# Splitting the first blocks' exponentials by slot under a new issue order, in a gated linear recurrence with an MLP mixer

## The chip, the cores and the metric

The kernel runs on one core of a Trainium2 chip. The metric is device time in microseconds (us) of the whole launch. Before the change it was 166.19 us, the median of three runs (165.96 to 166.21).

## What is computed

For each of 4 batches and 8 heads a 48 by 48 state is carried over 768 positions, and its output feeds a mixer of two matrix pairs, the first over positions ("token"), the second over the 384 features ("channel"):

```python
for t in range(S):                                   # S = 768
    state = alpha[:, :, t, :, None] * state + np.einsum('bhd,bhe->bhde', k[:, :, t], v[:, :, t])
    y[:, :, t] = np.einsum('bhd,bhde->bhe', q[:, :, t], state)
x = y as (batch, 768, 8 * 48)
h = np.maximum(x.transpose(0, 2, 1) @ w_tok1, 0.0) @ w_tok2
u = x + h.transpose(0, 2, 1)
out = u + np.maximum(u @ w_ch1, 0.0) @ w_ch2
```

## The kernel before, in words

**Blocks.** Each batch has 768 positions, worked in three blocks of 256, so there are 12 blocks, numbered 0 to 11. A block lies on 128 partitions in two slots: partition p holds positions 2p (slot 0) and 2p + 1 (slot 1) of all heads. For each block four loads of 384 KB fetch alpha (`ld_at`), k (`ld_kt`), q (`ld_qt`) and v (`ld_vt`). They go into 20 buffers called `in`. Six further pieces each of `wc1` and `wc2`, and two each of `wt1` and `wt2`, are the mixer's weights. They are fetched into the same buffers (`ldw_...`) and cast to bf16 (`cw_...`).

**The recurrence of a block.** ScalarE (ACT) takes the logarithm of alpha. TensorE (PE) multiplies it by triangular matrices, which gives running sums in PSUM (`cumw` for the first three blocks, `cum` for the others). ACT takes their exponential E and the exponential IE of the negative. q times E (`qq` for slot 1, `ql` for slot 0; tile pkq) and k times IE (`kk`, `kl`; tile pkk) are made on VectorE (DVE) or GpSimd (POOL). PE transposes both (`trq`, `trk`), an engine copies them out of PSUM (`evq`, `evk`), PE multiplies them (`G0_`, `G1_`), DVE applies the causal mask while it copies out (`mask0_`, `mask1_`; tile gtm, line 720), and PE multiplies by v (`y0_`, `y1_`). The state comes in by `K`, `sa`, `s0_`/`sm` and `ia`/`ib`. The result is copied to `x0_`, `x1_`. `vb` and `vs` cast v. The blocks 0, 1 and 2 (`WIDE` in the code) take both slots through the sums. The others first multiply the two slots of alpha (`P`) and need `lnP`, `ln1`, `r1`, `k0a` and `q0r`.

**The mixer of a batch.** When the three blocks of a batch have given six x tiles, come `t1` (token, first matrix), `ht` (relu), `t2`, `u` (adding x), a transpose of u (`up`/`ut` on PE for batches 0 and 1, a transposing DMA `ux` for 2 and 3), 24 groups `c1` of three matmuls, each with its relu `rt` on ACT or DVE, 24 groups `c2`, an add `o` on DVE, and a store `st`. In the last batch one output tile is cut into 320 columns (`h0`) and 64 columns (`h1`).

**What sets the order.** All operations, their engine and the order on each engine stand in one table of names, `ORDER`, and the buffers in a second table, `BUFS`. The last letter of an entry is its engine: t PE, s ACT, v DVE, g POOL, y SyncE (SP), which only issues DMAs. ACT issues those with the letter s. Every engine works through its entries in order, so an entry that waits holds all behind it. A method `shared` adds one more wait: where DVE and POOL take turns in a marked list of operations (products, casts and copies between SBUF tiles, in the table's order), the first on the new engine waits for the last on the other.

**Unread products.** Entries `f1_...` and `f3_...` are one or three matmuls of zeros into a bank that the named operation overwrites afterwards. Nothing reads them.

Of the kernel before, what the change touches and what calls it, by code (L numbers as in the profile page):

```python
# [380 lines left out]
kk2g vs0_1g ldw_wt11s y1_0t evq2v G0_1t ia1t kk3g f1_G11t ldw_wt20y ldw_wt21y mask0_1v k0a3g x1_0s G1_1t ld_kt4y vb2s
trk2t mask1_1v ldw_wc10y r13s ib1t K2t evk2s sa0_2t sm0_2v G0_2t cw_wt10s mask0_2v kl3g ldw_wc11y vs1_1g vs0_2g vs1_2s
ka3s vb3s f3_G12t G1_2t kb3s ldw_wc13y t1_0_1_0t y0_1t trk3t ld_at5y y1_1t cw_wt11g ib2t ia2t ln14s mask1_2v y0_2t
x0_1v x0_2v x1_1s vs1_3s vs0_3s ld_qt4s ldw_wc12y kc3g t1_0_1_1t y1_2t t1_0_0_0t t1_0_1_2t P4g t1_0_0_1t t1_0_0_2t
t1_0_0_3t t1_0_0_4t q0r3g x1_2v t1_0_0_5t t1_0_1_3t evk3v qq3g t1_0_1_4t ql3g lnP4s t1_0_1_5t k0a4g ht_0_0s cw_wt20s
K3t ht_0_1v cum4t cw_wt21s t2_0_0t t2_0_1t IE4s s0_3v sa1_3v u_0_0v t2_0_2t kk4g ldw_wc15y trq3t u_0_1v u_0_2v t2_0_3t
t2_0_5t kl4g E4s evq3s up_0_0t t2_0_4t u_0_3v cw_wc10s u_0_5v u_0_4v up_0_1t ut_0_1s ut_0_0v ld_vt4y G1_3t G0_3t
up_0_2t ib3t mask0_3v mask1_3v trk4t ldw_wc14y c1_0_0_0t c1_0_1_0t cw_wc11g ut_0_2s c1_0_2_0t c1_0_3_1t r14s cw_wc13s
ldw_wc21y c1_0_7_1t evk4s y1_3t y0_3t rt_0_1_0v q0r4v ka4v qq4v ql4g x0_3s x1_3v rt_0_0_0v rt_0_2_0v P5g cw_wc15g
c1_0_7_0t c1_0_6_1t rt_0_7_0s rt_0_7_1s cw_wc12s rt_0_3_1s c1_0_0_1t ld_qt5y c1_0_6_0t trq4t c1_0_2_1t c1_0_4_1t  # L390
ld_kt5y ldw_wc22y sm1_3g cw_wc14g vb4g lnP5s c1_0_10_1t evq4s ldw_wc20s rt_0_0_1s rt_0_6_0v rt_0_6_1v ld_vt5s
rt_0_2_1s c1_0_11_1t c1_0_11_0t rt_0_10_1v cum5t rt_0_11_1v G0_4t G1_4t kb4s IE5s rt_0_4_1v cw_wc21g kc4g ln15s E5s
c1_0_10_0t c1_0_3_0t r15s rt_0_10_0s c1_0_9_1t vs1_4g ldw_wc23y mask0_4v rt_0_9_1s rt_0_11_0s mask1_4v ldw_wc24y
c1_0_8_0t c1_0_4_0t c1_0_8_1t ia4t q0r5v vs0_4s y0_4t rt_0_8_0s rt_0_4_0s c1_0_1_1t c1_0_5_0t K4t c1_0_9_0t ldw_wc25s
rt_0_5_0s qq5v rt_0_8_1s x0_4s rt_0_9_0s cw_wc22s rt_0_3_0v rt_0_1_1v trq5t c1_0_5_1t ld_at6y k0a5g sa0_4v cw_wc20v
kk5v sm0_4v vb5v sa1_4v c2_0_5_0t c2_0_2_0t trk5t c2_0_1_0t c2_0_1_1t evq5s ib4t kc5g rt_0_5_1s cw_wc24g c2_0_2_1t
c2_0_5_1t evk5v sm1_4v P6g G0_5t ld_kt6s G1_5t cw_wc25g vs0_5s cw_wc23s y1_4t x1_4s c2_0_2_2t c2_0_1_2t ld_at7y
mask0_5v t1_1_1_0t ln16s r16s lnP6s c2_0_5_2t ia5t y0_5t c2_0_5_3t mask1_5v ld_qt6y K5t P7g sa0_5v ln17s x0_5s
t1_1_1_1t vs1_5g sm0_5v t1_1_1_2t t1_1_1_3t cum6t ld_kt7y ld_qt7y t1_1_1_4t k0a6v t1_1_0_0t lnP7s IE6s E6s o_0_5v
q0r6v c2_0_1_3t ib5t y1_5t t1_1_0_1t t1_1_0_2t cum7t ld_vt6y t1_1_0_3t x1_5s t1_1_0_4t k0a7g t1_1_1_5t kk6g t1_1_0_5t  # L400
# [492 lines left out]
```

## Time and profile before

| | before |
|---|---|
| device time, median of 3 runs | 166.19 us |
| device time of the profiled execution | 166.85 us |
| its span, first to last instruction | 165.1 us |
| busy: PE, DVE, ACT, POOL | 155.1, 111.3, 101.5, 74.4 us |
| read from HBM, written | 25.17 MB, 4.72 MB |

The profile is of one execution. A row of its timeline gives the start in us from the span's start, the length in us, the engine, the line, the operation with output and inputs, and in brackets the idle time ahead of it with what ended it. SPq and ACTq are the queues from which SP and ACT issue DMAs. A row of a stretch gives each engine's busy time and its count, the granted clock of PE as a share of full speed, the DMA engines' share and their rate. A row of a group gives the busy time, the mean ns of one, and the idle time ahead.

### The profile page before, as it was taken

Reading aid. Unit: us, or ns where it says so; the run is one execution under the profiler, and the core shown is the slowest. Engines: PE = TensorE matmul, PEld = TensorE weight load, DVE = VectorE, ACT = ScalarE, POOL = GpSimd, SP = SyncE. Lnnn points to the kernel's source line nnn. Section 1 sums busy time; section 2 is a strip of 40 time slices with the busy share of each in tenths; the row PEclk is TensorE's granted clock in tenths of the full one; section 3 lists DMA queues with packets and bytes.
Section 4 is the critical chain, followed back from the end, with each engine's and each line's share of the span. In section 5 each row is a group of like instructions: output and inputs, shape, how many; then the busy total and the mean of one; then the engine's idle time right before and its main releaser. Section 6 shows DMA issues by size and latency. Waiting matters only on the chain.

```text
span 165.1 us, 4068 instructions
## 1 busy us (share of the span) xinstructions
PE 155.1 (94%) x1601; PEld 98.2 (59%) x1601; DVE 111.3 (67%) x198; ACT 101.5 (61%) x188; POOL 74.4 (45%) x93
## 2 busy tenths in 40 slices
PE   7959689899999999999999999999899999999992
PEld 2543566486657676666667666665466565666660
DVE  4146699799699776967889999873582273624341
ACT  3788599998998787379977947465515101562000
POOL 4041769982942827289795384838700000000000
PEclk9996999999999999999999999999999999999999
DMA  5999999999999998999799999799012135220314
GB/s 130 317 301 296 269 322 297 305 353 347 343 361 342 308 284 206 276 310 157 158 315 205 247 136 239 136 214 255 7 48 99 48 59 131 95 97 4 113 75 143
DMA packets 76322, 34.46 MB, mean 209 GB/s; under 512 B 68112, under 2 KB 76304, under 8 KB 76304
## 3 DMA queue, kind: packets, MB, share of 16 engines
q1 hardware_dynamic: 64704, 27.73, 66.7%
q10 hardware_dynamic: 11600, 6.49, 13.0%
q8 instruction: 12, 0.20, 0.5%
q14 instruction: 6, 0.05, 0.1%
HBM read 25.17 MB, written 4.72 MB: 181 GB/s over the span
## 4 chain that ended last, share of the span: by engine, by line
PE 70%; DMA 9%; ACT 6%; POOL 5%; SPq 4%; DVE 2%; issue 2%; ACTq 0%; POOLq 0%; DVEq 0%
PE ps L834 28%; PE ps L829 21%; PE ps L604 10%; DMA in<-in_alpha_dram 6%; PE ps L810 5%; PE ps L805 4%; SPq L545 3%; DMA in<-in_v_dram 3%; POOL pkk L653 2%; PE ps L666 2%; PE ps L821 1%; POOL vb L698 1%; DVE rt L802 1%; ACT kt L697 1%; ACT vb L697 1%
## 5 line engine op out<-in xcount | busy, mean ns | idle before, releaser
L834 PE MATMUL ps<-wc,rt 128*128 128x384 bf16 (+2 forms) x300 | 54.7, 320 | 0.0
L829 PE MATMUL ps<-ut,wc 128*128 128x384 bf16 x288 | 51.7, 326 | 0.2 <-ACT E L631 0.2
L800 ACT ACTIVATE rt<-ps 128x384 bf16<-128x384 f32 x55 | 25.3, 493 | 25.2 <-PE ps L829 24.9
L829 PEld LDWEIGHTS <-wc 128*128 128x128 bf16 x288 | 27.1, 98 | 17.4 <-issue 0.5
L834 PEld LDWEIGHTS <-rt 128*128 128x128 bf16 x300 | 27.6, 98 | 16.5
L802 DVE TENSOR_SCALAR rt<-ps 128x384 bf16<-128x384 f32 x41 | 21.6, 552 | 14.0 <-PE ps L829 13.5
L720 DVE TENSOR_TENSOR gtm<-ps,mk 128x1024 bf16<-128x1024 f32 x24 | 28.3, 1216 | 3.2 <-PE ps L604 3.0
L838 DVE TENSOR_TENSOR o<-ps,u 128x384 f32<-128x384 f32 (+2 forms) x25 | 13.3, 535 | 6.1 <-PE ps L834 6.0
L653 POOL TENSOR_TENSOR pkk<-in,IE 128x384 bf16<-128x384 f32 (+1 forms) x10 | 12.3, 1242 | 8.0 <-DVE pkq L653 6.0
L814 DVE TENSOR_TENSOR u<-ps,x 128x384 bf16<-128x384 f32 x24 | 12.3, 552 | 4.2 <-PE ps L810 4.1
L653 POOL TENSOR_TENSOR pkq<-in,E 128x384 bf16<-128x384 f32 (+1 forms) x9 | 12.2, 1362 | 5.9 <-ACT tpk L697 3.2
L698 POOL CAST vb<-in 64x384 bf16<-64x384 f32 (+1 forms) x17 | 9.5, 558 | 10.4 <-issue 3.2
L697 ACT CAST x<-ps 128x384 bf16<-128x384 f32 x19 | 9.0, 480 | 8.1 <-PE ps L604 8.1
L697 ACT CAST vb<-in 64x384 bf16<-64x384 f32 (+1 forms) x18 | 11.8, 657 | 2.6 <-DMA in<-in_v_dram 1.2
L805 PE MATMUL ps<-x,wt 128*128 128x384 bf16 x48 | 11.4, 326 | 0.1
L810 PE MATMUL ps<-ht,wt 128*128 128x384 bf16 x48 | 10.1, 326 | 0.7 <-ACT wt L697 0.7
L589 POOL TENSOR_TENSOR in<-in 128x384 f32<-128x384 f32 x9 | 9.0, 999 | 3.8 <-DMA in<-in_alpha_dram 2.8
L604 PE MATMUL ps<-zs 128*128 128x512 bf16 x28 | 9.4, 469 | 1.1 <-DVE zs L507 1.1
L653 DVE TENSOR_TENSOR pkq<-in,E 128x384 bf16<-128x384 f32 (+1 forms) x8 | 5.6, 707 | 7.1 <-ACT E L637 4.2
L645 POOL TENSOR_TENSOR in<-in,in 128x384 f32<-128x384 f32 x7 | 7.0, 998 | 5.5 <-DVE in L649 3.0
L768 DVE TENSOR_TENSOR tmp<-ps,ss 128x384 f32<-128x384 f32 x12 | 6.7, 554 | 3.9 <-POOL ss L771 2.2
L604 PE MATMUL ps<-tpq,tpk 48*64 48x128 bf16 (+1 forms) x288 | 8.5, 221 | 0.3 <-ACT tpk L697 0.2
(93 smaller groups left out, 213.2 us busy)
## 6 DMA issues: line engine op xcount, KB each, us to landing
in<-in_alpha_dram SPq DMA_DIRECT2D x11, 384.0 KB, 5.6
in<-in_q_dram SPq DMA_DIRECT2D x10, 384.0 KB, 5.4
in<-in_moe_w_ch_dram SPq DMA_DIRECT2D x10, 384.0 KB, 6.9
in<-in_k_dram SPq DMA_DIRECT2D x9, 384.0 KB, 5.7
in<-in_v_dram SPq DMA_DIRECT2D x9, 384.0 KB, 5.4
out_dram<-o SPq DMA_DIRECT2D x14, 192.0 KB, 2.4
out_dram<-o ACTq DMA_DIRECT2D x9, 192.0 KB, 1.9
in<-in_moe_w_tok_dram SPq DMA_DIRECT2D x3, 384.0 KB, 5.7
```

Of the source, the lines that this page charges most:

```text
L604: return self.pe.matmul(out, lhsT=lhsT, rhs=rhs, start=start, stop=stop, skip_group_check=True)
L653: self.shared(self.eng[e].tensor_tensor(self.t(dst)[:, c : c + z, :, 0:D], self.t(src)[:, :, c : c + z, :].rearrange("p h s d -> p s h d") ...
L697: return self.act.copy(d, s)
L720: self.nc.vector.tensor_tensor(self.t(gtm)[:, hf, :, :], self.pair(gp).rearrange("p a (j t) -> p (a j) t", t=128), bass.AP(tensor=m.tensor ...
L800: self.act.activation(d, s, AF.Relu)
L802: self.nc.vector.tensor_scalar_max(d, s, 0.0)
L805: self.pe.matmul(self.bank(bank)[:, 0:HD], lhsT=self.wt1[:, kc, m * 128 : m * 128 + 128], rhs=self.t(x), start=(kc == 0), stop=(kc == NS - 1))
L810: self.pe.matmul(self.bank(bank)[:, 0:HD], lhsT=self.wt2[:, kc, i * 128 : i * 128 + 128], rhs=self.t(hts[kc]), start=(kc == 0), stop=(kc = ...
L814: self.nc.vector.tensor_tensor(self.t(u)[:, i % 3], self.bank(bank)[:, 0:HD], self.t(x), ALU.add)
L829: self.pe.matmul(self.bank(bank)[:, 0:HD], lhsT=self.wc1[:, kc, mc * 128 : mc * 128 + 128], rhs=self.t(ut)[:, 3 * half : 3 * half + 3, kc, ...
L834: self.pe.matmul(self.bank(bank)[:, 0 : cz - ca], lhsT=self.t(rts[mc][0])[:, i * 128 : i * 128 + 128], rhs=self.wc2[:, mc, ca:cz], start=( ...
L838: self.nc.vector.tensor_tensor(self.t(o)[:, ca:cz], self.bank(bank)[:, 0 : cz - ca], self.t(u)[:, i % 3, ca:cz], ALU.add)
```

## The change

The two instructions of a wide block that made E and IE for both slots (768 columns) become four of 384 columns, slot 1 (`E`, `IE`) and slot 0 (`Eb`, `IEb`). Each of the products waits only for its own slot's half. The tables `ORDER` and `BUFS` are replaced. The computation is the same. There are 958 entries in place of 947: six more exponentials, and the unread products change from twelve entries with 28 matmuls in all (13 of them before block 0's sums) to seventeen entries with 33 (12 before block 0's sums).

```diff
-            e1 = O("E", act(768), 4, writes=[E], reads=[cb], preds=[cum], emit=lambda e: g.exps(E, cb, 1.0))
+            e1, e2 = ({sl: O(nm + x, act(384), 4, writes=[v], reads=[cb], preds=[cum],
+                             emit=lambda e, v=v, f=f, sl=sl: g.exps(v, cb, f, sl)) for sl, x in ((1, ""), (0, "b"))}
+                      for v, nm, f in ((E, "E", 1.0), (IE, "IE", -1.0)))
             et = O("Et", act(16), 6, writes=[E], reads=[cb], preds=[cum], emit=lambda e: g.exptot(E, cb))
-            e2 = O("IE", act(768), 3, writes=[IE], reads=[cb], preds=[cum], emit=lambda e: g.exps(IE, cb, -1.0))
...
+        def need(x, sl):
+            return [x[i] for i in sl] if isinstance(x, dict) else [x]
...
-                      preds=(pre if 0 in sl else raw) + ([e2] if f is IE else [e1]),
+                      preds=(pre if 0 in sl else raw) + need(e2 if f is IE else e1, sl),
...
 ORDER = """
-f3_trk0t f1_trq0t f3_trq0t f3_cumw1t f3_cumw0t ld_at0y ln0s ld_at1y ln1s ld_qt0y ld_kt0y ld_vt0y cumw0t E0s ql0v
+ld_at1y f1_trq0t f1_trk0t f1_cumw0t f3_trk0t f3_trq0t f3_cumw0t ld_at0y ln0s cumw0t ln1s ld_kt0y ld_qt0y ld_at2s
...
-    def exps(self, E, cb, scale):
-        self.act.activation(self.t(E)[:, 0 : 2 * HD].rearrange("p (s c) -> p s c", s=2), self.pair(cb)[:, :, 0:HD],
-                            AF.Exp, scale=scale)
+    def exps(self, E, cb, scale, sl):
+        self.act.activation(self.t(E)[:, sl * HD : sl * HD + HD], self.bank(cb, sl)[:, 0:HD], AF.Exp, scale=scale)
```

**First place, the start.** On SP, before, the first loads were these (in_75 is alpha of block 0, in_77 alpha of block 1):

```order
L545 DMA in_75<-in_alpha_dram 128x8x96
L545 DMA in_77<-in_alpha_dram 128x8x96
L545 DMA in_69<-in_q_dram 128x8x96
L545 DMA in_67<-in_k_dram 128x8x96
L545 DMA in_75<-in_v_dram 128x8x96
```

Now on SP, in_69 is alpha of block 1 and in_68, behind it, alpha of block 0:

```order
L550 DMA in_69<-in_alpha_dram 128x8x96
L550 DMA in_68<-in_alpha_dram 128x8x96
L550 DMA in_76<-in_k_dram 128x8x96
L550 DMA in_82<-in_q_dram 128x8x96
L550 DMA in_64<-in_v_dram 128x8x96
```

Alpha 1 is first, alpha 0 second, and k 0 stands ahead of q 0. On ACT, before, the first work was this (la is the logarithm; E_90 and IE_91 are of block 0, IE_92 and E_88 of block 1):

```order
L598 ACTIVATE la_85<-in_75 128x16x48
L598 ACTIVATE la_84<-in_77 128x16x48
L637 ACTIVATE E_90<-ps 128x768
L637 ACTIVATE IE_91<-ps 128x768
L637 ACTIVATE IE_92<-ps 128x768
L641 ACTIVATE E_90<-ps 128x16
L697 COPY vb_99<-in_75 128x768
L637 ACTIVATE E_88<-ps 128x768
```

Now on ACT (E_88 and IE_91 are of block 0, E_89 and IE_92 of block 1):

```order
L603 ACTIVATE la_84<-in_68 128x16x48
L603 ACTIVATE la_85<-in_69 128x16x48
L550 DMA in_81<-in_alpha_dram 128x8x96
L642 ACTIVATE E_88<-ps 128x384
L642 ACTIVATE IE_91<-ps 128x384
L550 DMA in_67<-in_q_dram 128x8x96
L642 ACTIVATE E_88<-ps 128x384
L645 ACTIVATE E_88<-ps 128x16
L642 ACTIVATE IE_91<-ps 128x384
L645 ACTIVATE E_89<-ps 128x16
L701 COPY vb_100<-in_64 128x768
L642 ACTIVATE E_89<-ps 128x384
```

Block 0's logarithm stays first, its exponentials are in halves, and ACT now issues the loads of alpha 2 and q 1 between them.

**Second place, the products of blocks 0 and 1 and the first masks.** On DVE, before (pkq is q times E, pkk k times IE, tpq a copy out of PSUM, ss the state, gtm the masked product):

```order
L653 TENSOR_TENSOR pkq_93<-in_69,E_90 128x8x48 x2
L698 COPY tpq_106<-ps 128x2x512
L762 TENSOR_TENSOR ss_114<-ps,E_90 128x384
L653 TENSOR_TENSOR pkk_96<-in_66,IE_92 128x8x48 x2
L653 TENSOR_TENSOR pkq_93<-in_81,E_88 128x8x48
L762 TENSOR_TENSOR ss_112<-ps,E_90 128x384
L720 TENSOR_TENSOR gtm_108<-ps,mk 128x1024 x2
```

Now on DVE (tpk_104 is `evk0`, which was ACT's before):

```order
L657 TENSOR_TENSOR pkq_93<-in_82,E_88 128x8x48
L657 TENSOR_TENSOR pkk_97<-in_76,IE_91 128x8x48 x2
L766 TENSOR_TENSOR ss_112<-ps,E_88 128x384
L702 COPY tpk_104<-ps 128x1024
L702 COPY tpq_106<-ps 128x2x512
L657 TENSOR_TENSOR pkk_95<-in_68,IE_92 128x8x48
L766 TENSOR_TENSOR ss_115<-ps,E_88 128x384
L724 TENSOR_TENSOR gtm_109<-ps,mk 128x1024
L657 TENSOR_TENSOR pkq_94<-in_67,E_89 128x8x48 x2
L724 TENSOR_TENSOR gtm_109<-ps,mk 128x1024
```

DVE takes over k's two products of block 0, which were POOL's, and the copy `evk0`, and it makes q's two products of block 1 between the two masks of block 0. POOL makes `qq0` and `kl1` instead, then `P3`.

**Third place, the end.** On DVE, before, the last additions into the output tiles (o) were these:

```order
L838 TENSOR_TENSOR o_155<-ps,u_130 128x384
L838 TENSOR_TENSOR o_153<-ps,u_131 128x64
L838 TENSOR_TENSOR o_156<-ps,u_130 128x384
L838 TENSOR_TENSOR o_154<-ps,u_131 128x320
L888 UnconditionalBranch
```

Now on DVE:

```order
L842 TENSOR_TENSOR o_155<-ps,u_128 128x384
L842 TENSOR_TENSOR o_156<-ps,u_130 128x384
L842 TENSOR_TENSOR o_154<-ps,u_130 128x320
L842 TENSOR_TENSOR o_153<-ps,u_130 128x64
L892 UnconditionalBranch
```

The tile of 64 columns comes last in place of the tile of 320. Its store is issued by ACT, the one of 320 by SP.

Further along, the same operations stand in another order on every engine. `vb11` and `kc11`, late in the recurrence, go from POOL and DVE to ACT. The set of PE's operations ahead of the first `t2` of batch 0 is the same, apart from the unread products.

More of the change, by code (lines that the diff above doesn't have):

```diff
@@ L381 @@
[L381 to L400, printed above, removed]
@@ new lines @@
+rt_0_5_0s mask1_4v c1_0_9_0t c1_0_5_1t x0_4v rt_0_3_0v ld_at7s c1_0_1_1t ld_at6s kc4s rt_0_4_0v qq5v rt_0_8_1s
+rt_0_5_1s rt_0_1_1s K4t c1_0_8_0t k0a5v rt_0_9_0s rt_0_10_0s trq5t c2_0_2_0t rt_0_8_0s cw_wc22s c2_0_1_0t sa0_4v
+ldw_wc25y kk5v ld_kt6y ld_at8y sm0_4v vb5g trk5t evq5s c2_0_1_1t sa1_4v ib4t c2_0_2_1t y1_4t ld_qt7y evk5v G0_5t
+ld_vt6s vs1_5v cw_wc23s sm1_4g cw_wc24g x1_4v G1_5t mask1_5v mask0_5v kc5g cw_wc25g c2_0_5_0t t1_1_1_0t ln17s vs0_5s
+t1_1_1_1t t1_1_1_2t t1_1_1_3t c2_0_5_1t c2_0_1_2t c2_0_2_2t K5t sa0_5v ia5t P6g y0_5t t1_1_0_0t x0_5v lnP6s sm0_5g
@@ new lines @@
+t1_1_0_1t c2_0_1_3t c2_0_5_2t t1_1_1_4t c2_0_0_0t o_0_1v cum6t ib5t y1_5t t1_1_0_2t c2_0_5_3t c2_0_0_1t t1_1_0_3t
+x1_5v t1_1_1_5t t1_1_0_4t t1_1_0_5t ld_kt7y o_0_5v P7g r17s ht_1_0v k0a6g c2_0_3_0t c2_0_3_1t IE6s P8v kk6v lnP7s E6s
+ht_1_1s t2_1_5t c2_0_0_2t q0r7g k0a7g u_1_5v c2_0_3_2t t2_1_1t cum7t t2_1_2t t2_1_3t u_1_1v u_1_2v c2_0_4_0t t2_1_0t
+u_1_3v c2_0_4_1t t2_1_4t vb6s ld_vt7s u_1_0v up_1_1t u_1_4v ut_1_1v up_1_0t ln16s c2_0_4_2t c2_0_0_3t ut_1_0v
+c2_0_4_3t st_0_5s IE7s E7s vs0_6s r16s vs1_6s up_1_2t ld_qt6y ld_at9y ln18s ka6s lnP8s kk7g kb6g qq7g ut_1_2v
@@ L442 @@
+o_3_4v o_3_5v c2_3_3_2t c2_3_2_2t c2_3_0h0_0t st_3_1s c2_3_3_3t c2_3_2_3t c2_3_0h0_1t o_3_3v st_3_4s st_3_3y o_3_2v
+c2_3_0h0_2t c2_3_0h0_3t st_3_5s o_3_0h0v c2_3_0h1_0t c2_3_0h1_1t c2_3_0h1_2t st_3_2s st_3_0h0y c2_3_0h1_3t o_3_0h1v
+st_3_0h1s
 """
 BUFS = """
[11 rows of a table removed]
[11 rows of a table added]
 """
```

98 lines of the change are left out of this document (53 added, 45 removed), and 22 rows, old and new, of the table BUFS.

## The prediction

> **What bounds the kernel now.** I read the page first, for the busy shares and the chain that ended last, then the table of stretches, then the timeline of the start and of two later places. From the page, the span, the engines, and the chain by engine:
>
> ```profile
> span 165.1 us, 4068 instructions
> PE 155.1 (94%) x1601; PEld 98.2 (59%) x1601; DVE 111.3 (67%) x198; ACT 101.5 (61%) x188; POOL 74.4 (45%) x93
> PE 70%; DMA 9%; ACT 6%; POOL 5%; SPq 4%; DVE 2%; issue 2%; ACTq 0%; POOLq 0%; DVEq 0%
> ```
>
> PE carries 70% of the chain. The rest lies in few places, which the stretches show (busy PE, PEld, DVE, ACT, POOL, then the granted clock):
>
> ```profile
> 8.00:12.00 4.00, 2.30 (x44) 1.66 (x43) 1.92 (x3) 3.54 (x8) 1.95 (x2) 0.95 1.12 303
> 12.00:16.00 4.00, 4.00 (x33) 1.67 (x34) 2.71 (x6) 3.36 (x6) 0.50 (x1) 0.62 1.12 297
> 28.00:32.00 4.00, 3.29 (x44) 2.05 (x40) 3.33 (x8) 3.92 (x9) 3.85 (x5) 1.00 0.97 283
> 36.00:60.00 24.00, 23.84 (x259) 16.01 (x258) 20.46 (x33) 21.53 (x42) 13.46 (x18) 1.00 1.10 332
> 60.00:98.00 38.00, 38.00 (x426) 24.80 (x425) 32.29 (x55) 28.85 (x55) 26.10 (x26) 1.00 1.10 234
> 98.00:120.00 22.00, 21.19 (x235) 13.15 (x237) 15.01 (x26) 12.85 (x26) 14.20 (x17) 1.00 0.72 160
> ```
>
> From 36 to 162 us PE stands still for 0.16 us in the first stretch, 0.81 in the last shown, and nearly nothing else. So the kernel is a front, in which loads and the other engines decide, a PE stream of fixed length, and a tail. In 28 to 32 us ACT and POOL are the full ones (3.92 and 3.85 of 4). The front ends where the second token product of batch 0 starts:
>
> ```profile
> 31.23 1.55 ACT L697 CAST wt<-in 128x768 bf16<-128x768 f32 x2
> 32.10 1.15 PE L810 MATMUL ps<-ht,wt 128*128 128x384 bf16 x6 [0.67 <-ACT wt L697]
> ```
>
> It starts at 32.10, released by a weight cast on ACT. As the same PE operations lie ahead of it before and now, the change is worth the shift of that start, plus what changes in later stalls and in the tail.
>
> **Term 1, the start.**
>
> ```profile
> 0.81 1.08 SPq L545 DMA_DIRECT2D in<-in_alpha_dram  x2
> 4.27 0.84 ACT L598 ACTIVATE la<-in 128x768 bf16<-128x768 f32 x1 [2.19 <-DMA in<-in_alpha_dram]
> 5.48 0.84 ACT L598 ACTIVATE la<-in 128x768 bf16<-128x768 f32 x1 [0.36 <-DMA in<-in_alpha_dram]
> 5.69 0.65 PE L604 MATMUL ps<-la,u 128*128 128x384 bf16 x3
> 6.75 0.81 ACT L637 ACTIVATE E<-ps 128x768 f32<-128x768 f32 x1 [0.42 <-PE ps L604]
> 7.45 0.81 ACT L637 ACTIVATE IE<-ps 128x768 f32<-128x768 f32 x1
> 9.60 0.83 ACT L697 CAST vb<-in 128x768 bf16<-128x768 f32 x1 [0.23 <-DMA in<-in_v_dram]
> 14.78 0.56 DVE L653 TENSOR_TENSOR pkq<-in,E 128x384 bf16<-128x384 f32 x1 [1.24 <-DMA in<-in_q_dram]
> ```
>
> The first load landed at 4.27, the second at 5.48, v 0 as the fifth at 9.60, q 1 as the ninth at 14.78. That is (14.78 - 4.27)/8 = 1.31 us a load, so the place in the queue decides when a load lands. Alpha 0, now second, lets its logarithm start at 5.48, not 4.27. Block 0's sums waited for unread products until 5.69. Now they wait for the logarithm, 5.48 + 0.84 = 6.32, and start **0.6 us later**.
>
> **Term 2, the halves.**
>
> ```profile
> L637 ACT ACTIVATE E<-ps 128x768 f32<-128x768 f32 x3 | 2.4, 809 | 0.5 <-PE ps L604 0.4
> 21.77 0.52 ACT L631 ACTIVATE E<-ps 128x400 f32<-128x400 f32 x1
> 22.15 0.51 ACT L634 ACTIVATE IE<-ps 128x384 f32<-128x384 f32 x1
> ```
>
> The row of 384 columns takes 0.51 us where the whole takes 0.81, and the next one starts 0.38 us later (21.77 to 22.15), where after a whole it was 0.70 (6.75 to 7.45). Six more instructions cost ACT 6 x (2 x 0.38 - 0.70) = 0.36 us, by lengths alone 6 x (2 x 0.51 - 0.81) = 1.3. I take 0.36, since ACT runs them back to back. The first half is there 0.30 us before the whole would be.
>
> The Trainium skill, page "ScalarE: Activation LUTs", section "Rules for kernel authors", budgets about 0.3 us for each ACTIVATE beside its elements, which speaks against the split. By it the six would cost 1.8 us of ACT, and the sum below would come out 1.4 us worse. The rows above give 0.21 us as that fixed part (384 more columns cost 0.30, and 0.51 - 0.30 = 0.21), and 0.06 where such instructions follow each other, so the trace does not agree.
>
> **Term 3, the front's walk.** These rows of the timeline are the old path from block 0's products to the last mask of block 2, with one row of unread products (zs) and two of groups for later use:
>
> ```profile
> 7.59 1.03 DVE L653 TENSOR_TENSOR pkq<-in,E 128x384 bf16<-128x384 f32 x2 [4.25 <-ACT E L637]
> 8.76 1.95 POOL L653 TENSOR_TENSOR pkk<-in,IE 128x384 bf16<-128x384 f32 x2 [6.02 <-DVE pkq L653]
> 9.11 1.30 DVE L698 COPY tpq<-ps 128x1024 bf16<-128x1024 bf16 x1 [0.49 <-PE ps L666]
> 14.28 0.61 PE L604 MATMUL ps<-tpq,tpk 48*128 48x128 bf16 x8
> 20.36 0.81 PE L604 MATMUL ps<-zs 128*128 128x512 bf16 x3
> 15.72 2.34 DVE L720 TENSOR_TENSOR gtm<-ps,mk 128x1024 bf16<-128x1024 f32 x2
> 17.08 0.99 POOL L589 TENSOR_TENSOR in<-in 128x384 f32<-128x384 f32 x1 [2.80 <-DMA in<-in_alpha_dram]
> L697 ACT CAST x<-ps 128x384 bf16<-128x384 f32 x19 | 9.0, 480 | 8.1 <-PE ps L604 8.1
> L697 ACT CAST vb<-in 128x768 bf16<-128x768 f32 x8 | 6.7, 840 | 1.7 <-DMA in<-in_v_dram 1.2 <-POOL in L645 0.4
> 25.66 2.36 DVE L720 TENSOR_TENSOR gtm<-ps,mk 128x1024 bf16<-128x1024 f32 x2
> 29.32 0.68 DVE L698 COPY tpk<-ps 128x1024 bf16<-128x1024 bf16 x1
> ```
>
> The walk, with these lengths. The sums end 6.32 + (6.75 - 5.69) = 7.38. The halves of block 0 then come at 7.9, 8.3, 8.7 and, after an issued load, near 9.5. q 0, now fourth, lands at 4.27 + 3 x 1.31 = 8.2. DVE makes `ql0` to 8.75, `kk0` to 9.3 and, waiting for the last half, `kl0` to 10.05. Before, k's products ended on POOL at 10.71, so the split and the move to DVE win **0.65 us** here in spite of term 1. Then DVE does more in a row: the state, behind v 0's cast (from 9.60 on) and PE's sums of k and v, to an estimated 12.1, `evk0` (0.68) to 12.8, `evq0` (1.30) to 14.1. G of block 0 starts at 14.15, against 14.28. The three unread products ahead of it, at (0.81 - 0.16)/3 = 0.22 each, end by 14.55 if they start with the end of the sums of block 2, which is hidden, because DVE first does `kk1` and a state and is free at 15.2. `mask0_0` starts there, 0.5 us before 15.72. But `qq1` and `ql1` (1.1) now precede `mask1_0`, which ends at 18.7, against 18.06. By the shared rule `P3` on POOL waits for `ql1`: 17.55, against 17.08. `lnP3` and all behind it on ACT follow 0.5 us late, block 1's and 2's copies `evk` among them. From 18.7 on DVE has three states and two x copies (0.55 each, as the products), `evq2` (1.30) and two pairs of masks (2.34 and 2.36): 8.75, to 27.45, and with an estimated 0.6 of waits for those copies the last mask ends at 28.05, against 25.66 + 2.36 = 28.02. **The masks are level.** What is left is ACT's list between the cast of `wt1` and that of `wt2`. It reaches the first 0.5 us late, as all behind `lnP3`. Gone from there to the other engines, or to behind it, are a v cast of 768 columns (0.84) and a logarithm, a copy of k and a relu of 384 columns, which I put at the x copies' 0.48 each: 2.28. Three x copies have come from DVE: 1.44. So ACT is 0.84 shorter, less the 0.5: t2 at 31.7, **0.4 us earlier**, with the relus done by then on DVE. Bounds: 1.2 us earlier, if ACT's list follows without the 0.5 and DVE's waits shrink by as much (30.9), and 0.9 us later, if terms 1 and 3's delay of `P3` are both carried to the end (0.6 + 0.5, less 0.2 that the halves gain).
>
> The five extra unread products cost 5 x 0.22 = 1.1 us of PE if nothing covered them. PE's idle 1.7 us in 8 to 12 and the clock of 0.62 in 12 to 16 lie in the front, where PE waits for others, so I count them and a better clock at nothing.
>
> **Term 4, the stream.** The stall of 0.81 us:
>
> ```profile
> 109.36 0.58 SPq L545 DMA_DIRECT2D in<-in_v_dram  x1
> 113.81 1.39 POOL L698 CAST vb<-in 128x768 bf16<-128x768 f32 x2 [0.38 <-DMA in<-in_v_dram]
> 117.98 0.34 PE L604 MATMUL ps<-vb,pkk 128*128 128x96 bf16 x4 [0.81 <-DVE o L838]
> ```
>
> v 11 lands 4.4 us after its issue. Its casts sit behind it, a DVE copy behind those, an output add behind that, and `K11` needs that add's bank. Now `vb11` and `kc11` are ACT's, and one more `c1` group (0.49) lies between, so the stall can go. The new order can also stall elsewhere. The nearest size for that is this row: I allow two stalls of 0.8, so +1.6 to -0.97 (all 0.81 + 0.16 gone), and take **-0.2**.
>
> **Term 5, the tail.**
>
> ```profile
> 161.88 0.49 DVE L838 TENSOR_TENSOR o<-ps,u 128x320 f32<-128x320 f32 x1 [0.67 <-PE ps L834]
> L838 DVE TENSOR_TENSOR o<-ps,u 128x64 f32<-128x64 f32 x1 | 0.2, 224 | 0.1
> out_dram<-o SPq DMA_DIRECT2D x1, 160.0 KB, 1.8
> out_dram<-o SPq DMA_DIRECT2D x1, 32.0 KB, 1.6
> ```
>
> The last add is now 64 columns, 0.22 in place of 0.49, and its store lands in 1.6 in place of 1.8: **-0.45**. The 320-column add runs beside the last 12 narrow matmuls. Bounds -0.2 (the big store becomes last) and -0.65.
>
> **Sum.** 165.1 - 0.4 - 0.2 - 0.45 = 164.05 us of span. The profiled execution took 166.85, 1.75 beyond its span, so this is 165.8 for such an execution. It stood 0.66 above the median of the runs, so from the median 166.19 - 1.05 = **165.1 us**.
>
> **Rivals.** *The turns of DVE and POOL cost the front* (slower). `kk1` on DVE waits for `kl1` on POOL (1.00 us), which needs k 1 and the last half of block 1. It decides if k 1, sharing the engines with the loads that ACT issues, lands after 13.1, as `kl1` then ends after 14.1, when DVE gets to `kk1`. Everything to `ql1`, `P3` and `lnP3` moves, up to 0.9 later at t2: 0.9 - 0.45 - 0.1 = +0.35, **166.5**. For it speaks that the ninth load landed at 14.78, against it that k 1 is sixth on SP. *ACT is blocked late* (slower): `vb11` waits on ACT for v 11, with relus behind it, the banks fill and PE stops, 1.6 us: -0.4 - 0.45 + 1.6 = +0.75, **166.95**. For it, the 4.4 us of that load; against it, PE has some 20 groups of 0.49 in between. *The loads hold the stream*: with DMA at 1.10 through 60 us, an earlier t2 only meets its weights earlier, and the front's gain is given back: 166.19 - 0.45 = **165.75**, or 166.0 with the small tail gain. Against it, no DMA wait shows behind PE there now.
>
> **Chances.** Forecast and better 0.50, turns 0.20, blocked ACT 0.12, loads 0.18 (of which 0.11 within 0.2%, or 0.33 us, about what a measurement of this kernel can tell from no change, and 0.07 faster). So faster 0.57, same 0.11, slower 0.32. The bounds alone reach from 163.4 to 168.5; ends that need every term at its bound are left out, which leaves 163.8 to 167.3.
>
> **What would show it.** Alpha 0's logarithm near 5.5, k's products of block 0 done by 10.1, `P3` near 17.5, last mask of block 2 near 28.0, t2 at 31.7, no PE wait over 0.3 at `K11`, and a last add of 64 columns with some 2.8 us behind PE's end in place of 3.26. A t2 after 32.5, or PE waits over 1 us in all between 36 and 160, would make it wrong.

## The result, and the profile after

The changed kernel takes **170.5 us** (median of four executions, 170.12 to 171.26) where the kernel before takes 166.2 (four, 165.96 to 166.86). The ratio is 1.0258, with a 95% interval of 1.0212 to 1.0304: it is slower. The forecast was 165.1 us with a range up to 167.3, so sign and range were both wrong; 170.5 also lies beyond 168.5, which the prediction's bounds reach together. Single executions differ, those of the kernel before by up to 1% from their median, those of some kernels below by more, so medians carry the argument. The ratios leave out executions that took over 1.5% longer than the fastest of their kernel, so a ratio can lie below that of the medians, most of all for g4, where three of six are left out.

The profiled execution took 170.12 us, with a span of 168.4 where before had 165.1. These are the page's span, its engines and the chain of work that ended last, by engine:

```profile
span 168.4 us, 4082 instructions
PE 157.1 (93%) x1606; PEld 98.8 (59%) x1606; DVE 117.3 (70%) x209; ACT 93.3 (55%) x181; POOL 77.2 (46%) x95
PE 65%; DMA 14%; ACT 8%; DVE 5%; issue 2%; ACTq 2%; SPq 1%; POOL 1%; DVEq 0%
```

ACT has 8 us less to do than before (93.3 for 101.5), and still DMA and ACTq, the queue from which ACT issues loads, have grown in the chain (9% to 14%, 0 to 2%). PE's own part fell from 70% to 65%. Next the stretches, in the columns used before (busy PE, PEld, DVE, ACT, POOL, granted clock):

```profile
8.00:12.00 4.00, 3.79 (x52) 2.39 (x50) 2.59 (x6) 3.97 (x11) 1.41 (x2) 1.00 1.17 325
28.00:32.00 4.00, 2.44 (x18) 1.28 (x18) 1.37 (x3) 3.00 (x7) 2.37 (x4) 0.88 1.13 351
32.00:36.00 4.00, 4.00 (x35) 2.65 (x33) 3.20 (x7) 3.52 (x7) 1.80 (x3) 0.69 1.12 338
36.00:60.00 24.00, 22.63 (x251) 15.00 (x250) 20.77 (x35) 18.45 (x33) 13.22 (x18) 1.00 1.06 317
98.00:120.00 22.00, 21.76 (x264) 13.84 (x263) 17.41 (x28) 11.37 (x24) 14.82 (x16) 1.00 1.00 195
```

The early front is better (PE 3.79 for 2.30 in 8 to 12 us, with the clock at 1.00), and so is 98 to 120. Two stretches are worse. In 28 to 32, where ACT had been full, it works 3.00 of 4 and PE 2.44, and the granted clock then falls to 0.69. In 36 to 60, PE stands still for 1.37 us where it stood for 0.16.

The timeline of the start shows that the forecast walk was followed, and beaten:

```profile
5.44 0.84 ACT L603 ACTIVATE la<-in 128x768 bf16<-128x768 f32 x1 [3.36 <-DMA in<-in_alpha_dram]
6.33 0.65 PE L609 MATMUL ps<-la,u 128*128 128x384 bf16 x3 [1.22 <-ACT la L603]
7.18 0.49 ACT L642 ACTIVATE E<-ps 128x384 f32<-128x384 f32 x1 [0.17 <-PE ps L609]
7.57 0.48 ACT L642 ACTIVATE IE<-ps 128x384 f32<-128x384 f32 x1
14.09 1.21 DVE L724 TENSOR_TENSOR gtm<-ps,mk 128x1024 bf16<-128x1024 f32 x1
16.31 0.99 POOL L594 TENSOR_TENSOR in<-in 128x384 f32<-128x384 f32 x1 [3.71 <-DVE pkq L657]
24.78 2.35 DVE L724 TENSOR_TENSOR gtm<-ps,mk 128x1024 bf16<-128x1024 f32 x2
```

The last mask of block 2 ends at 24.78 + 2.35 = 27.13, against 28.02 before. At that point the change is 0.9 us ahead of the profiled execution of before (which ran late there, as the section on the prediction shows). The next rows, of the timeline from there to the second token product, show where it falls behind:

```profile
25.85 0.51 ACT L701 COPY kt<-pkk 64x384 bf16<-64x384 bf16 x1
27.85 0.96 ACTq L572 DMA_DIRECT2D in<-in_moe_w_ch_dram  x2
28.90 0.86 ACT L701 CAST x<-ps 128x384 bf16<-128x384 f32 x2 [2.55 <-DMA in<-in_q_dram]
29.43 0.48 PE L809 MATMUL ps<-x,wt 128*128 128x384 bf16 x2 [1.77 <-ACT x L701]
33.29 1.69 PE L814 MATMUL ps<-ht,wt 128*128 128x384 bf16 x6
```

ACT ends its copy at 26.36 and does nothing until 28.90. In its list the loads of `wc10` and `wc11` stand between the copy and the casts of x. They are issued only at 27.85 to 28.81, and the casts cannot pass them. (The bracket names a load of q as what ended the idle time. That is inferred by the profile; the list of semaphores below shows what the two loads wait for.) PE waits 1.77 us for the first of these x tiles. The second token product starts at 33.29 (before 32.10, forecast 31.7), and its first six matmuls take 1.69 us, at the lower clock, in place of 1.15. The same happens again later:

```profile
49.98 3.09 ACTq L550 DMA_DIRECT2D in<-in_alpha_dram  x2
53.11 0.51 ACT L701 COPY pkk<-pkk 64x384 bf16<-64x384 bf16 x1 [2.64 <-issue]
53.68 0.34 PE L609 MATMUL ps<-vb,pkk 128*128 128x96 bf16 x4 [1.10 <-ACT pkk L701]
```

The loads of alpha 7 and 6 take 3.09 us to issue, ACT is idle for 2.64 of them, `kc4` (the copy) and five relus stand behind them, and PE waits 1.10 us ahead of `K4`. These are the semaphores for which the loads wait in the built program, between the instructions before and behind them on ACT (DMAHW0 to 7 count loads that have landed, and the others count work of the named engine):

```
L701 TensorCopy kt_98<-pkk_96 64x8x48 [waits Pool_49]
L572 DMACopy in_68<-in_moe_w_ch_dram 128x3x256 [waits DMAHW7_49]
L572 DMACopy in_82<-in_moe_w_ch_dram 128x3x256 [waits DMAHW3_49,DMAHW1_49]
L701 TensorCopy x_118<-ps 128x384 [waits DVE_49,PE_49]
...
L804 Activation rt_141<-ps 128x384 [waits DVE_49,PE_49]
L550 DMACopy in_73<-in_alpha_dram 128x8x96 [waits DMAHW3_49]
L550 DMACopy in_65<-in_alpha_dram 128x8x96 [waits DMAHW5_49,Activation_49,Pool_49]
L701 TensorCopy pkk_97<-pkk_97 64x8x48
```

All four wait for earlier loads to land; the last waits for readers of its buffer too. Issued from SP, which only issues DMAs, such a wait holds only other DMAs (in e1 below, SP takes 4.50 us from 23.86 on to issue three weight loads, and ACT's casts go on meanwhile); issued from ACT it holds ACT's arithmetic. The Trainium skill, page "DMA: Bandwidth & Descriptors", section "Issuing engines are not separate DMA queues", says that issuing from several engines saves only the sequencer time of issuing. Here the choice of engine also decided what stood still behind a load that was not yet allowed to go.

The tail, from the timelines of DVE and PE, and PE's last row in the kernel before:

```profile
164.96 0.63 DVE L842 TENSOR_TENSOR o<-ps,u 128x320 f32<-128x320 f32 x2 [0.66 <-PE ps L838]
157.76 7.51 PE L838 MATMUL ps<-wc,rt 128*128 128x384 bf16 x57
```

```profile
155.73 6.11 PE L834 MATMUL ps<-wc,rt 128*128 128x384 bf16 x41
```

The adds of 320 and of 64 columns run back to back, 0.63 us for both, so the short last add starts only behind the long one. PE ends at 157.76 + 7.51 = 165.27, before at 161.84. The longer span thus divides: the start of the second token product +1.19 (33.29 against 32.10), the stream from there to PE's end +2.24, the time behind PE's end -0.13 (3.13 against 3.26), together +3.3. The medians lie 4.3 apart, because the profiled execution of before was 0.66 above its median and that of the changed kernel 0.38 below.

### The profile page after: what moved, and what is told of

It is laid out like the page before. It is cut to its first block, busy times and chain, and to the rows that moved or that the text cites. A ratio compares the mean times of both kernels' runs of the same rounds, so it can differ in the third digit from the quotient of the medians.

```text
span 168.4 us, 4082 instructions
## 1 busy us (share of the span) xinstructions
PE 157.1 (93%) x1606; PEld 98.8 (59%) x1606; DVE 117.3 (70%) x209; ACT 93.3 (55%) x181; POOL 77.2 (46%) x95
## 4 chain that ended last, share of the span: by engine, by line
PE 65%; DMA 14%; ACT 8%; DVE 5%; issue 2%; ACTq 2%; SPq 1%; POOL 1%; DVEq 0%
PE ps L838 25%; PE ps L833 20%; PE ps L609 10%; DMA in<-in_alpha_dram 7%; DMA in<-in_k_dram 4%; PE ps L814 4%; PE ps L809 4%; DVE gtm L724 3%; DMA ut<-u 3%; PE ps L825 1%; ACTq L550 1%; ACT rt L804 1%; PE ps L670 1%; ACT x L701 1%; ACT vb L701 1%
## 5 line engine op out<-in xcount | busy, mean ns | idle before, releaser
L833 PE MATMUL ps<-ut,wc 128*128 128x384 bf16 x288 | 50.7, 326 | 0.4 <-DMA ut<-u 0.2
L804 ACT ACTIVATE rt<-ps 128x384 bf16<-128x384 f32 x51 | 23.4, 493 | 29.9 <-PE ps L833 28.2
L806 DVE TENSOR_SCALAR rt<-ps 128x384 bf16<-128x384 f32 x45 | 22.9, 550 | 8.4 <-PE ps L833 8.4
L701 ACT CAST vb<-in 64x384 bf16<-64x384 f32 (+1 forms) x24 | 14.8, 616 | 0.4
L775 POOL TENSOR_TENSOR ss<-tmp,E 128x384 bf16<-128x384 f32 x9 | 7.5, 836 | 6.2 <-DVE tmp L772 4.0
L702 POOL CAST vb<-in 64x384 bf16<-64x384 f32 (+1 forms) x11 | 6.8, 620 | 6.9 <-DVE ss L775 5.7
L609 PEld LDWEIGHTS <-gtm 128*128 128x128 bf16 x192 | 7.8, 96 | 2.8 <-issue 0.9
L702 DVE CAST x<-ps 128x384 bf16<-128x384 f32 x13 | 7.2, 551 | 3.2 <-PE ps L609 3.2
L701 ACT CAST x<-ps 128x384 bf16<-128x384 f32 x11 | 5.1, 478 | 7.5 <-PE ps L609 4.3
L609 PE MATMUL ps<-vb,gtm 128*128 128x48 bf16 x192 | 8.7, 183 | 0.3 <-POOL vb L702 0.3
```

The costliest lines, as they stand in the source:

```text
L609: return self.pe.matmul(out, lhsT=lhsT, rhs=rhs, start=start, stop=stop, skip_group_check=True)
L701: return self.act.copy(d, s)
L702: return self.shared(self.eng[e].tensor_copy(d, s))
L804: self.act.activation(d, s, AF.Relu)
L806: self.nc.vector.tensor_scalar_max(d, s, 0.0)
L833: self.pe.matmul(self.bank(bank)[:, 0:HD], lhsT=self.wc1[:, kc, mc * 128 : mc * 128 + 128], rhs=self.t(ut)[:, 3 * half : 3 * half + 3, kc, ...
```

## The experiments

**Theory A**: ACT's list is stopped at loads that may not be issued yet, at the two places above, and that is the price. **Rivals**: the data arrive late, wherever they are issued; or the new order costs time by itself (alpha 1 first, the turns of DVE and POOL, the split, the tail). Entries with y are issued by SP, those with s by ACT. Buffers stay as they were for each value.

### e1: the weights of the first place on SP

```diff
-ldw_wc10s ldw_wc11s
+ldw_wc10y ldw_wc11y
```

> The changed kernel with the two loads of the channel weights' first pieces (ldw_wc10, ldw_wc11) issued by SP instead of ACT. Theory A (ACT stands still behind a load that may not be issued yet: ACT idle 2.55 us at 26.4, PE idle 1.77 us ahead of its third t1 matmul, then a lower clock): t2 of batch 0 starts at 31.0 to 31.7 in place of 33.29, device time down by about 1.8, to 168.7. Rival B (loads arrive too late whoever issues them, and the order is simply DMA-bound there): no change, 170.5 within 0.4.

Measured: 168.25 us (168.04 to 170.55), ratio to before 1.0191 [1.0105, 1.0276], with before at 165.86 on that chip. The time came down by 2.25 us, but not all by theory A. The stop was gone, and the casts of x followed the copy at once. PE then waited for the cast of the second token weight (`wt2`), and that for its data, by the timelines of ACT and PE:

```profile
31.24 0.83 ACT L701 CAST wt<-in 128x768 bf16<-128x768 f32 x1 [1.47 <-DMA in<-in_moe_w_tok_dram]
32.12 1.15 PE L814 MATMUL ps<-ht,wt 128*128 128x384 bf16 x6 [1.88 <-ACT wt L701]
```

So the second token product started at 32.12, and not at 31.0 to 31.7 as expected. At the first place late data are a second limit, close behind the stop. PE's wait ahead of `K4` was shorter too, 0.42 in place of 1.10, although the loads of the second place had not been moved.

### e2: alpha 7 and 6 on SP

```diff
-ld_at7s ... ld_at6s
+ld_at7y ... ld_at6y
```

> The changed kernel with the loads of alpha 7 and alpha 6 issued by SP instead of ACT. Theory A (ACT idle 2.64 us until 53.11, the copy kc4 and five relus behind it, PE idle 1.10 us ahead of K4): that PE wait goes, device time down by about 1.1, to 169.4. Rival B: no change, 170.5 within 0.4.

Measured: 166.84 us (165.84 to 168.26), ratio 1.007 [1.0031, 1.0108]. That is 3.7 us less by the medians, where 1.1 was expected. In the profiled execution the wait ahead of `K4` is gone. But at the first place too, which this edit does not touch, ACT stood still for 1.40 us in place of 2.55, PE waited 1.13 in place of 1.77, and PE's clock stayed at 1.00. So the length of a stop differs from one execution to another, and the gain of e2 is not that of the second place alone.

### e3: all four on SP

```diff
-ldw_wc10s ldw_wc11s ... ld_at7s ... ld_at6s
+ldw_wc10y ldw_wc11y ... ld_at7y ... ld_at6y
```

> The changed kernel with those four loads issued by SP. Theory A: both gains add up, 2.9 us, to 167.6, still above the kernel before, as further parts of the 4.3 us are open. Rival B: no change, 170.5 within 0.4.

Measured: 167.3 us (165.96 to 169.65), ratio 1.0089 [1.0049, 1.0128], near the expected 167.6. The two gains do not simply add up, though: PE again waits for the second token weight (1.49 us, the second token product starts at 32.56), and e2 alone came as low.

### e4: all of ACT's 23 loads on SP

```diff
-ld_at2s ld_qt1s ld_at4s ldw_wt21s ld_kt4s ldw_wc10s ... ld_qt11s
+ld_at2y ld_qt1y ld_at4y ldw_wt21y ld_kt4y ldw_wc10y ... ld_qt11y
```

> The changed kernel with all 23 loads of ACT issued by SP, in the table's order. Theory A: no load holds ACT any more, at least the gain of the four loads, 167.0 to 167.6, unless SP, which then issues every load, transpose and most stores in order, holds loads back behind one that waits (rival C, SP becomes the one that is held: 168 or more with DMA waits in place of ACT's). Rival B: 170.5 within 0.4.

Measured: 166.12 us (165.46 to 167.28), ratio 1.0031 [0.9997, 1.0066]. So 4.4 of the changed kernel's us by the medians, or 3.8 by the two ratios, go when the same order has its loads on SP. Two stretches of e4, and the rows of its timeline from ACT's cast of `wt1` to the second token product:

```profile
28.00:32.00 4.00, 3.56 (x41) 2.11 (x38) 3.27 (x7) 3.90 (x9) 2.78 (x4) 1.00 1.11 359
36.00:60.00 24.00, 24.00 (x253) 16.04 (x251) 21.54 (x34) 17.95 (x34) 15.02 (x20) 1.00 1.08 320
```

```profile
25.59 0.82 ACT L701 CAST wt<-in 128x768 bf16<-128x768 f32 x1
...
26.97 0.51 ACT L701 COPY kt<-pkk 64x384 bf16<-64x384 bf16 x1
27.50 0.86 ACT L701 CAST x<-ps 128x384 bf16<-128x384 f32 x2
...
31.64 1.15 PE L814 MATMUL ps<-ht,wt 128*128 128x384 bf16 x6 [0.29 <-ACT wt L701]
```

The casts of x now follow the copy with no pause, PE has no idle time from 36 to 60, and the second token product starts at 31.64, 1.65 us before that of the changed kernel. It stands within 0.1 us of the forecast 31.7. Rival C, that SP is the one held up, does not show in the time. Moving four loads (e3) does not do better than moving two (e2): their intervals overlap widely.

### f1: the kernel before, with alpha 6 and 7 on ACT

```diff
-ld_at6y ... ld_at7y
+ld_at6s ... ld_at7s
```

> The kernel before with one thing of the change put in: the loads of alpha 6 and alpha 7 issued by ACT at the same place of the table. SP needed 3.02 us for these two at 45.39, where a free issue takes 0.37. Theory A (ACT stands behind a load that may not be issued yet): ACT stands 1.5 to 2.6 us there, relus behind it, PE waits, 1 to 2.3 us slower than the kernel before. Rival B (the loads are late whoever issues them): within 0.4 of the kernel before.

Measured: 171.88 us (170.6 to 173.45), ratio 1.0354 [1.0311, 1.0396]. Two loads moved, nothing else, cost 6.1 us, where 1 to 2.3 or nothing was expected. And they do not stop ACT: they are issued in 0.37 and 0.38. What the timeline of ACT shows is this:

```profile
50.42 0.37 ACTq L545 DMA_DIRECT2D in<-in_alpha_dram  x1
55.69 0.38 ACTq L545 DMA_DIRECT2D in<-in_alpha_dram  x1
62.21 0.52 ACT L592 ACTIVATE lf<-in 128x384 f32<-128x384 f32 x1 [4.60 <-DMA in<-in_alpha_dram]
```

In the kernel before, SP's timeline has both out by 45.39 + 3.02 = 48.41:

```profile
45.39 3.02 SPq L545 DMA_DIRECT2D in<-in_alpha_dram  x2
```

In f1 the second load goes out at 55.69, because ACT's arithmetic stands ahead of it. Its logarithm waits 4.60 us, and in turn PE, by its table of waits (us in total, times, longest), waits for the x tiles:

```profile
PE ps L805 <- ACT x L697: 4.4, 2, 4.1
```

These 4.4 us are most of the 5.0 by which the profiled spans differ (170.1 and 165.1). That is a second mechanism, a load late behind arithmetic, and theory A alone had not said it.

### f2, f3, f4: parts of the change in the old order

f2 is the changed code under the old tables, with `Eb` and `IEb` beside `E` and `IE`; f3 puts alpha 1 ahead of alpha 0; f4 exchanges the halves of the last tile.

```diff
-E0s
+Eb0s E0s
...
-ld_at0y ln0s ld_at1y ln1s
+ld_at1y ld_at0y ln0s ln1s
...
-c2_3_0h1_0t ... o_3_0h1v st_3_0h1y ... c2_3_0h0_0t ... o_3_0h0v st_3_0h0s
+c2_3_0h0_0t ... o_3_0h0v st_3_0h0y ... c2_3_0h1_0t ... o_3_0h1v st_3_0h1s
```

> The kernel before with the exponentials of the first three blocks in halves, slot 0's beside slot 1's, and the old tables otherwise. By the prediction's own term (six times 0.06 us of ACT, the first half 0.3 us earlier): within 0.4 of the kernel before. By 0.3 us for each added instruction: up to 1.4 slower. A gain over 0.4 would mean that the halves themselves feed the front.

> The kernel before with the load of alpha 1 issued ahead of alpha 0, nothing else. Block 0's logarithm starts at 5.45 in place of 4.27, its sums 0.6 later. If the front's later waits take that up: within 0.3 of the kernel before. If it is carried to the end: 0.6 slower.

> The kernel before with the 320-column part of the last output tile ahead of the 64-column part. The prediction's tail term: 0.45 faster (bounds 0.2 to 0.65). The changed kernel's trace (adds back to back, 3.13 us from PE's end to the span's end in place of 3.25): 0.1 faster, which these runs can't tell from nothing.

Measured, with before at 165.75 on that chip: f2 165.41, ratio 0.9994 [0.9963, 1.0024]; f3 166.53, 1.0062 [1.0035, 1.009]; f4 166.25, 1.0019 [0.9985, 1.0053]. The split alone and the tail alone make no difference that can be told from none. Alpha 1 first costs the old order 0.6%, about 1.0 us. The 1.4 us of f2's second expectation, 0.3 us for each added instruction, did not come, as its interval ends at +0.24%, or 0.4 us.

### g1: e4 with alpha 0 first again

```diff
-ld_at1y ... ld_at0y ln0s cumw0t ln1s
+ld_at0y ld_at1y ... ln0s cumw0t ln1s
```

> The changed kernel with all 23 loads issued by SyncE, and alpha 0 loaded ahead of alpha 1 again. Theory (ScalarE's issues cost 4.4 us, alpha 1 first costs 1.0 of its own): about 1.0 below the kernel with all loads on SyncE alone, 165.1 us, 0.4 per cent under the kernel before. Rival (the 1.0 that alpha 1 first cost the old order belongs to that order, since the new one has the k products of block 1 ahead of those of block 0): no gain, 166.1 or above, because the rest of the list stands for alpha 1 first.

Measured: 166.73 us (165.81 to 167.8), ratio 1.0073 [1.0033, 1.0114], with before at 165.47. It is no faster than e4. So the 1.0 us of f3 belongs to the old order, and is not a part of what the changed kernel lost.

### g2: the kernel before with all its 12 ACT loads on SP

```diff
-ldw_wt11s ld_qt4s ldw_wc20s ld_vt5s ldw_wc25s ... ld_kt10s
+ldw_wt11y ld_qt4y ldw_wc20y ld_vt5y ldw_wc25y ... ld_kt10y
```

> The kernel before with its 12 ScalarE loads issued by SyncE. Theory (a load on ScalarE costs where it is held at issue or late; in the kernel before none was): within 0.3 per cent of before, 165.5 to 166.3 us. Rival (moving loads off ScalarE is a gain in any order, so that it is no property of the change): about half of the 4.4 us for half as many loads, 163.6 us.

Measured: 168.51 us (166.23 to 168.86), ratio 1.0154 [1.0106, 1.0203]. Both expectations were wrong: the old order loses about 2.5 us by it. So in that order these 12 loads are better issued by ACT. The profiled execution was the one of 166.23, the fastest of six, so no trace shows where the others lost time, and this stays open.

### g3 and h4: alpha 7 and 6 late on SP

Both are e4 with those two loads further back in SP's list; in h4 they are behind k 6.

```diff
-ld_at7y c1_0_1_1t ld_at6y ... ldw_wc25y kk5v ld_kt6y
+c1_0_1_1t ... ldw_wc25y kk5v ld_kt6y ld_at7y ld_at6y
```

> The changed kernel with all loads on SyncE, and alpha 7 and 6 there put behind the last weight load of the stage, so that they are issued near 51 us as ScalarE issued them, but hold nothing on ScalarE. Theory (what cost time in the second place was the hold on ScalarE's list, 2.64 us): at most 0.4 us over the kernel with all loads on SyncE, 166.1 to 166.5 us. Rival (these loads simply came too late): the 3 us or so between the changed kernel and the one with these two moved come back, 168 to 170 us, and the logarithms of alpha wait for data.

> The changed kernel with all loads on SyncE, and alpha 7 and 6 behind the keys of block 6 there, to be issued at 51.5 to 53 us, as late as ScalarE issued them in the changed kernel, with nothing held. Theory (the stop is the price): at most 0.4 us over the 166.1 without the move. Rival (lateness of the data): 168 to 170 us, and the logarithms of alpha wait for data by over 1 us.

Measured: g3 166.25 us, 1.0044 [1.0015, 1.0074]; h4 166.24 us (165.52 to 167.78), 1.0031 [1.0001, 1.0061]. g3 was a weak test, as its loads went out only 0.8 us later than those of e4. In h4 alpha 7, 6 and 8 go out between 49.96 and 55.70, and a logarithm does wait for its data, by the timelines of SP and ACT:

```profile
49.96 5.74 SPq L550 DMA_DIRECT2D in<-in_alpha_dram  x3
```

```profile
56.97 0.52 ACT L597 ACTIVATE lf<-in 128x384 f32<-128x384 f32 x1 [2.30 <-DMA in<-in_alpha_dram]
```

The time does not change against e4's 166.12. In this order the data may be that late; the rival of lateness falls for the second place. The profiled execution was the slowest of the twelve (167.78), and still its first token product of batch 1 starts at 55.39, beside 55.27 in e4. (In the old order, f1, it was the cause: there the wait was 4.60.)

### g4: only the four loads on ACT

e4, with `wc10`, `wc11`, alpha 7 and alpha 6 back on ACT.

```diff
-ldw_wc10y ldw_wc11y ... ld_at7y ... ld_at6y
+ldw_wc10s ldw_wc11s ... ld_at7s ... ld_at6s
```

> The changed kernel with 19 of its 23 ScalarE loads on SyncE; only the two weight pairs ahead of the copies of x (wc10, wc11) and alpha 7 and 6 stay on ScalarE. Theory (these four are the cost): 169 us or above, near the changed kernel's 170.5. Rival (the cost is spread over all 23, or needs the queue of loads ahead of these four on ScalarE, so that SyncE's issues make the lanes free earlier or later): 166.5 to 168 us.

Measured: 169.05 us median of six, ratio 1.0121 [1.0074, 1.0168]. The six lie apart: 166.30, 167.01 and 167.97, then 170.13, 170.18 and 170.95. The profile is of the fastest, and in it the four loads hold ACT for less, by the timeline of ACT:

```profile
24.40 1.83 ACTq L572 DMA_DIRECT2D in<-in_moe_w_ch_dram  x2
48.48 1.52 ACTq L550 DMA_DIRECT2D in<-in_alpha_dram  x2
50.04 0.51 ACT L701 COPY pkk<-pkk 64x384 bf16<-64x384 bf16 x1 [1.08 <-POOL in L653]
```

The issues of the first place end at 26.23, before the casts of x are due. The median of 169.05 is what the theory expected, but the fastest three are not: these four loads can cost nearly the whole loss, and need not. That the three executions above 170 are those with longer stops is likely and was not seen.

### h1, h2, h3: the stop alone

All loads are on SP, as in e4. ACT gets 16 small copies to a tile that nothing reads, where the loads stood: in h1 at the first place, in h2 at the second, in h3 at both.

```diff
+    def hold(self, n):
+        for _ in range(n):
+            self.act.copy(self.dum, self.zs)
...
             o.emit(o.on)
+            if o.name in ('ldw_wc11', 'ld_at6'):
+                g.hold(16)
```

> The changed kernel with all 23 loads on SyncE, and 16 small copies to an unread tile (about 2.6 us in all, an estimate from the 0.51 us rows of three times their size) on ScalarE where the two weight loads ahead of the copies of x stood. The copies are work that the reference does not have. Theory (the stop of ScalarE's list is the price): TensorE idles again ahead of the first products of the token mixer and the time rises by 1 to 2.6 us over the 166.1 without the stop. Rival (the late weights or the lanes were the price): under 0.5 us more.

> As h1, but the 16 copies stand where the loads of alpha 7 and 6 stood. Theory (the stop): the copy of the keys behind it and the relus are late, TensorE idles ahead of the state products of block 4, and the time rises by 1 to 2.6 us over 166.1. Rival (late alpha): under 0.5 us more.

> Both stops of h1 and h2 in one kernel. Theory (the stops, and nothing else, make the changed kernel slow): 169.5 to 171, as the changed kernel's 170.5. Rival (stops are caught up elsewhere): less than 167.

Measured, with before at 165.86: h1 172.24 us (172.01 to 173.72), 1.0408 [1.0369, 1.0446]; h2 171.17 (169.84 to 172.36), 1.0312 [1.026, 1.0364]; h3 178.13 (177.92 to 178.86), 1.0757 [1.0723, 1.079]. The times lie above the 1 to 2.6 us that were expected for one stop and the 169.5 to 171 for both. The stops came out twice as long as meant, which the rows of the timelines of h1 and h2 show, with PE's wait behind each:

```profile
27.45 5.24 ACT L614 COPY dum<-zs 128x128 bf16<-128x128 bf16 x16
33.28 0.80 PE L814 MATMUL ps<-x,wt 128*128 128x384 bf16 x2 [5.04 <-ACT x L706]
```

```profile
48.13 5.23 ACT L614 COPY dum<-zs 128x128 bf16<-128x128 bf16 x16
53.94 0.46 PE L610 MATMUL ps<-vb,pkk 128*128 128x96 bf16 x4 [3.59 <-ACT pkk L706]
```

Of a stop of 5.24 us, 5.04 reach PE at the first place, and of 5.23 us 3.59 at the second, where PE has 1.64 us of other work. The whole time grows by 6.1 and 5.05 us, and by 12.0 for both, all over e4. That is more than PE's waits; behind each the granted clock is lower (0.66 from 32 to 36 us in h1, 0.75 and 0.82 from 52 to 60 in h2). So a stop with no load in it is enough, it is not given back later, and two stops cost about their sum (11.2). The second place also fits by size: 2.64 - 1.64 = 1.0 us should reach PE in the changed kernel, and 1.10 did.

## Why the prediction was wrong

**The miss, term by term.** The forecast span was 164.05 us, the measured one 168.4. Of the 4.35 between them the front (term 3) has 1.59 (33.29 for 31.7), the stream (term 4) 2.44 (+2.24 for -0.2) and the tail (term 5) 0.32 (-0.13 for -0.45).

**Term 1 and term 2 held.** Alpha 0's logarithm started at 5.44 (forecast 5.48), the sums at 6.33 (6.32), the halves 0.39 apart (0.38). The split alone is level (f2). The Trainium skill, page "ScalarE: Activation LUTs", section "Rules for kernel authors", gives the 0.3 us for a bias that is passed as a pointer; the built program passes a constant here, so the prediction took a figure that was not for these instructions.

**Term 3's masks were better than forecast.** The first mask started at 14.09 (forecast 15.2), `P3` at 16.31 (17.55), the last mask ended at 27.13 (28.05), 0.9 us earlier, where I had called them level. So the rival of the turns did not come. But the 0.9 us against the kernel before are partly luck of the draw. f1 and f4 leave the whole front as it was before, and in their profiled executions the last mask ended at 26.51 and 26.36, and the second token product started at 31.04 and, in f4, at

```profile
30.75 1.15 PE L810 MATMUL ps<-ht,wt 128*128 128x384 bf16 x6 [0.67 <-ACT wt L697]
```

So one and the same front differs by 1.35 us between executions, and the 32.10 from which the forecast counts was the latest of the three. The third rival, that an earlier start is given back later, does not hold between these two: in f4 the start is 1.35 earlier than in the profile of before, and PE ends 1.14 earlier (160.70 for 161.84).

**The step that failed is the last of term 3**, "What is left is ACT's list between the cast of `wt1` and that of `wt2`". I counted that list as casts, copies, a logarithm and a relu, found it 0.84 us shorter, and put t2 at 31.7. The list also holds three loads, of k 4, `wc10` and `wc11` (before it held one, q 4), and I priced them at nothing, although the change takes ACT from 12 loads to 23. With them on ACT the start is 33.29. With all loads on SP (e4) it is 31.64, the step's number, in part by luck, since e4's masks ended at 28.25 and not at 27.13. With `wc10` and `wc11` alone on SP (e1) it is 32.12, because the data of the second token weight are late. So the step left out two waits, that of a load's issue and, close behind it, that for this weight. The rival *ACT is blocked late* named the right kind of wait at another place: arithmetic that waits for landed data (`vb11`). It did not see that the issue of a load can itself wait, with all arithmetic behind it.

**Term 4 was mis-signed for the same reason.** Its stall did go: 0.19 ahead of `K11`, as this row of PE's timeline shows, and 0.24 elsewhere in 98 to 120, in place of 0.81:

```profile
121.90 0.33 PE L609 MATMUL ps<-vb,pkk 128*128 128x96 bf16 x4 [0.19 <-ACT vb L701]
```

The prediction allowed two new stalls of 0.8 as its bound, +1.6, and took -0.2; the stream grew by 2.24. The stop at alpha 7 and 6 costs 1.10 at `K4`, and the first six matmuls of the second token product lose 0.54 by the clock, for which the prediction had no term. Against e4 the path from the second token product to the first matmul of batch 1's mixer (59.24 - 33.29 = 25.95 in the changed kernel, 55.27 - 31.64 = 23.63 in e4) is 2.32 longer; 0.21 more of it is a wait for a relu, and the remaining 0.47 was not located. Together with the 1.65 us of the start that is the whole difference of the two spans, 168.4 - 164.5 = 3.9.

**Term 5** gave -0.13 in place of -0.45: with the 320-column add and the 64-column add back to back, the last add ends only a little sooner after PE. f4 shows no gain of it in the old order.

Both of the prediction's signs of being wrong came: the second token product after 32.5, and PE waits of over 1 us between 36 and 160 (1.37 from 36 to 60 alone).

**What stays open.** Without the stops the new order is level with the old one (e4, 166.12 beside 165.86), not 1.1 us better. The missing 0.32 of the tail is a part of that. Another is that the profiled execution of before, from which I subtracted, was long for its kernel (166.85; of 89 further executions, four were longer). Its second token product at 32.10 was late by the same measure: e4's 31.64 is 0.46 ahead of it, but 0.6 and 0.9 behind the 31.04 and 30.75 of f1 and f4. Why the old front differs so between executions, and why a stop in the changed kernel does (e2, g4), was not found. No kernel tried here beats the one before with an interval that excludes no change.

## What to carry to other kernels

When a change moves loads to an engine that also computes, list the loads in that engine's order with what each waits for, and price each as a possible stop for everything behind it, as one prices a slow instruction. The same holds the other way round: a load behind arithmetic goes out only when that arithmetic is done (f1, 6.1 us for two loads). Which engine issues a load is a matter of its neighbours, not of the engine: moving loads off ACT gained about 4 us in one order and lost about 2.5 in the other (e4, g2).
